# Second stage of a filter transform in groups of three columns, and a modulation vector formed later from another place

## The chip, the core and the metric

The kernel runs on one core of a Trainium2 chip, as one launch. The time is device microseconds of that core. TensorE (PE), VectorE (DVE), ScalarE (ACT), GpSimd (POOL) and SyncE (SP, here only a queue for transfers) each work through their own list of instructions, in the order in which the program emits them.

## What is computed

Two layers with a modulation taken from `c`, on 2048 positions of 640 channels, in bf16:

```
mod = (silu(c) @ w_mod) cut into sa, ca, ga, sb, cb, gb   (six vectors of 640)

h  = layernorm(x) * (1 + ca) + sa            x = A_q
ks = a causal convolution of k with 4 taps per channel (shift_k)
kv = ks * v
y  = irfft(rfft(kv, 4096) * rfft(ssm_k, 4096))[:2048] + kv * ssm_D
x  = x + ga * (h * y)

h  = layernorm(x) * (1 + cb) + sb
t  = gelu(layernorm(h) @ w1)                 640 -> 640
   shift the four quarters of t's channels by +1, -1, +2, -2 positions
x1 = h + t_shifted @ w2
o  = x1 + gelu(layernorm(x1) @ w3) @ w4      640 -> 1728 -> 640
x  = x + gb * o                              the result
```

`ssm_k` is called s below: s and kv go through the same transform, are multiplied, and go back.

## The kernel before, in words

**The long convolution.** The transform of length 4096 is done as small matrix products. For s and then for kv, 32x32 block transposes on DVE (L395) lay the data out, `stage1` (L408) makes products into T01, in two halves T0 and T1 (20480 columns in all), and stage 2 makes products of T01 with a table Gs in RG. Every stage-2 product goes to PSUM and is copied out (an eviction, by ACT at L208 or by DVE at L210), into R3 for s (called `KSX`) and into R5 for kv (`XS`). Then `inverse1` (DVE products of the two spectra at L633, matmuls at L644 and L645), `inverse2` (L685, which reads T01), and the result y in Rb.

The two stage 2 differ. That of s, `stage2` (L425), takes one column k of 32 at a time for both halves: 4 matmuls 128x320 (as 64 rows of the array at a time) into one PSUM slot and one eviction 128x640. That of kv, `stage2_half` (L446), takes one half at a time and three columns k: 12 matmuls of 160 columns and one eviction 128x960; the last of a half has two k, and 640.

**The modulation.** `mod_half` (L500 to L528) loads a 400 KB half of a column block of `w_mod`, makes its product with silu(c) (5 matmuls, L509), and puts 320 columns into `modv`. The halves i = 0 to 5 go by three early places; i = 6 to 11 (cb, then sb, then gb) use places `wl` in R3 at 0, 1600, ... 8000. The part of `modv` that holds cb, sb and gb is one region "modB", 6 to 12, to the bookkeeping.

**Second layer.** Positions are 16 tiles of 128, A0 to A15, in groups CG: [0], [1], [2], [3,4], [5,6], ... [13,14], [15] (so group 4 is A5 and A6). For a group, `chain_a` (L761 to L764) makes the new x with a sum, `chain_b` (L771 to L782, here "quick" at L775 for the first three groups, else L779 and L780) makes h, `chain_c` makes the normed h; each has a layer norm's end in `ln_finish` (L724 to L741, small POOL and DVE steps with a power on POOL at L739) and squares summed on ACT (L753). `turn` transposes a normed tile: by TensorE (L796 and a copy at L802 or L804) or, for later groups, by a DMA on SP's queue (L789, `R<-RK`). `mm_w1(g)` (L842 and L852) then multiplies a group by w1, `mm_w2` (L897, out at L904), `mm_w3` (L931, gelu at L935), `mm_w4` (L952 and L961) follow, with the output lines at L984 to L1006. `ln1_stats` and `ln1_fin` (L554 to L577) and `make_q` (L608 to L618) prepare h of the first layer tile by tile.

**Loads and places.** w3 (2160 KB, L1020) goes into the lower half of T01 and w4 (2080 KB, L1021, with two 80 KB tails at L1022 and L1023, these four in the program's order of tasks 494 to 497) into the upper half, when the transform no longer needs them. gelu's output sits in R3 (`gsf`), with zeroed edges from `gs_zero`.

**What sets the order.** `add` records a task with the regions that it reads and writes, and `run` puts all tasks in an order written out by hand, ORDER: every word is a task's number and its engine (P, A, D, G, S), and behind a colon the one to two of four PSUM slots that it takes, as in `88P:0`. Each engine gets its tasks in this order, SP's transfers too. So what is written next to what in ORDER decides who waits behind whom; the numbers given to a task as costs decide nothing at run time. A task starts when those that it depends on are done: regions that overlap, with a write among them.

Of the kernel before, what the change touches and what calls it, by code (L numbers as in the profile page):

```python
# [26 lines left out]
0S 2S 19G 18D 21G 20D 27G 29D 23D 4S 50G 28D 24A 36G 37G 22D 30A 68G 69D 25A 26G 88P:0 31A 89A 86P:1 87A 56G 90P:2 91A 72G 84P:3 5S 85A 3S 38G 39G 40A  # L27
73D 104P:0 106P:1 107A 70D 6S 49G 71D 105D 98P:2 102P:3 103A 99A 8S 118P:0 74G 94P:1 95A 75D 114P:3 115A 108P:2 109A 9S 119D 112P:0 113A 1S 66D 116P:1
41G 42G 43G 67D 80P:3 81A 117D 51D 52D 110P:2 44A 45D 10S 111D 96P:0 97A 82P:1 122P:3 11S 123D 32G 34G 54A 33S 53A 83A 76P:0 77A 100P:2 101D 92P:1 93A
78P:3 7S 120P:0 46G 136D 79A 55G 121D 175P:2 176A 47S 195P:1 196A 35S 179P:3 180A 185P:2 186D 147P:1 141P:0 193P:3 142D 148A 57G 58G 181P:2 182D 59G  # L30
139P:1 194A 140A 201S 199P:0 48S 200A 143P:3 144D 155P:2 165P:1 166D 156A 161P:0 162A 202S 191P:3 192D 12S 157P:2 158A 167P:1 168D 13S 163P:0 164A
197P:3 198A 145P:2 203S 146D 189P:1 65G 151P:0 152D 169P:3 190A 204S 183P:2 170A 184D 159P:1 160A 177P:0 178D 153P:3 154A 173P:2 174A 149P:1 150D
137P:0 260P:3 254D 171P:2 187P:1 138A 60A 188A 61G 62G 63G 261A 214D 172A 14S 124P:0 266P:1 210D 267A 125D 126P:3 127D 15S 211D 255D 209A 258P:2 259A
16S 270P:1 271A 130P:0 131D 268P:3 64A 262P:2 343G 269A 263A 215A 128P:1 264P:3 129D 256D 276P:2 277A 265A 134P:0 132P:1 17S 135D 282P:2 212A 283A
133D 216G 286P:3 223S 224P:0 220S 213G 278P:1 287D 225A 226S 279A 232S 284P:2 257D 221P:0 229S 285A 272P:3 227P:1 222A 228D 274P:2 235S 275D 273A
290P:0 291A 469D 288P:1 289A 233P:3 234D 292P:2 293A 294P:0 296P:3 230P:1 297A 298P:2 295D 299A 466D 342S 253G 246S 248G 312P:0 308P:3 309A 231D 463D
300P:1 301A 313D 460D 251G 310P:2 311D 367G 243S 306P:0 307A 316P:3 317D 280P:1 281A 252G 314P:2 304P:0 302P:3 305A 249S 240G 315D 236P:1 303A 237D
318P:2 319D 467D 340P:0 345D 241S 341A 338P:1 339A 238S 242G 326P:3 327A 344D 245S 250G 366S 322P:2 334P:0 352D 330P:1 331D 323A 244G 335A 239G 247G
324P:3 325A 346P:2 350S 351G 353D 347A 348P:0 360D 320P:3 349A 321A 328P:1 329A 354P:2 355A 359G 358S 361D 374S 356P:0 368D 369D 332P:3 333A 375G
362P:1 363A 364P:2 376D 365A 336P:3 337A 370P:1 371A 357A 372P:2 377D 378P:3 379A 380P:1 381A 383G 382S 385D 384D 386P:0 390S 391G 392D 393D 398S 373A  # L40
388P:3 387A 217A 399G 401D 394P:1 400D 425S 396P:2 397A 408D 407G 389A 402P:0 406S 409D 404P:2 395A 414S 416D 405A 415G 417D 464D 465D 426P:3 403A
427D 452S 410P:1 411A 412P:2 413A 420P:0 421D 418P:1 419A 422S 423P:3 456S 461D 470D 424D 468D 462D 218A 475P:20 477D 476A 520D 459G 454S 499D 500D
471D 521D 472A 540D 434S 219G 523D 541D 543D 437S 438P:1 439A 512A 435P:3 428S 429P:2 430A 431S 432P:0 501A 522A 433A 436A 525D 502G 504D 457S 478P:12
480A 503G 524G 526D 505D 473D 491P:03 545D 542A 544G 507D 553A 492A 527A 474D 546D 479A 571D 568D 485P:20 528G 529G 493A 530D 531P:1 506A 508G 509D
510P:3 486A 208S 547A 487A 458G 511A 548D 549G 481G 569D 570A 572D 573A 482P:20 484A 550D 551P:3 552A 532D 536P:1 533A 513D 537A 207S 574D 483D 575G
576D 580D 577D 517P:0 518A 581D 582D 583A 538P:3 578D 584G 579A 539A 585G 488P:21 489A 556P:0 557A 534D 535D 558P:3 559A 515P:2 516A 453S 514D 631D
632D 633A 586D 589D 590P:0 587P:3 455S 560P:2 634D 206S 635D 637G 591D 636A 638G 554D 561D 563D 588A 639D 562A 600P:0 601A 598P:3 599A 643D 640D 641D
642A 564G 494S 565D 644D 645D 646A 205S 441A 647D 490A 648G 566P:2 498G 567D 444D 651D 555D 605P:0 606D 607A 602P:3 649D 443D 603D 497S 652S 650S 699D
700D 447D 604A 620P:2 621A 495S 616P:1 617A 618P:0 661P:3 619A 662A 659P:2 660A 622P:1 623A 608D 609G 440D 610D 611P:0 613D 614P:3 615D 701A 663P:2
666P:1 664D 612A 683P:3 665A 667D 668A 681P:0 682A 677P:2 445G 656A 653D 654D 442G 655D 592D 669D 670G 674A 678A 671D 672P:1 673D 679P:0 680A 675P:1  # L50
593D 594D 702D 703D 496S 624P:2 595D 596D 676A 519G 597D 765D 749P:0 704A 705G 706G 766D 767A 768D 684A 707A 449A 625D 711D 747P:1 685P:32 712D 748A
769D 713D 714A 708D 709D 715D 771G 626D 446D 770A 710A 745P:1 716G 686P 717A 718S 772G 450D 719D 687D 720S 729P:3 773D 448G 750A 629S 774D 775D 777A
778D 779D 746A 727P:0 721D 781D 722D 723D 834D 835D 780A 776A 730A 627S 451G 790A 787A 657D 658D 782G 783D 743P:1 785D 791D 728A 731P:3 831D 832D 630S
688D 833A 732D 744A 733A 734P:0 735D 784S 786S 793P:1 794A 795P:3 737D 693D 694D 697S 736A 751P:02 796A 797P:1 800P:3 752P 738G 741D 836A 837G 838G
839D 753D 840D 798D 692S 739A 740S 742S 815P:0 843D 844D 801D 803D 841D 696S 813P:1 811P:3 845D 847G 842A 846A 848G 851D 788D 816A 849D 724A 725D 689S
809P:0 799A 852S 802A 804G 807D 814A 810A 812A 805D 850S 853P:1 759D 854A 808S 855P:2 856A 806S 875P:0 876A 869P:3 857P:1 873P:2 871P:0 726D 792D 874A
690S 789D 628S 754D 691S 891D 892D 894D 870A 860P:2 760D 951D 872A 895D 896A 695S 817P:30 893A 897G 898G 952D 954D 861D 862A 858D 863D 877P:21 953A
818P 903A 758S 904D 819D 899D 900D 698S 820D 859A 864G 865A 955G 905D 866S 906A 879D 822S 878P 867A 868S 933P:3 824S 901D 907G 902A 908G 909D 934A
911D 910S 956D 957D 958D 825D 912S 915P:2 935P:0 936A 913P:3 916A 763S 931P:0 757S 959A 914A 917P:2 929P:3 932A 960G 930A 961G 756S 821S 823S 962D
755S 963S 966P:0 967A 918D 919A 826D 885D 886D 920P:2 921D 830S 888S 829S 923G 762S 764S 922A 964P:1 965A 937P:30 969P:2 761S 880D 924G 968G 970D  # L60
972P:1 1003P:2 939D 925A 881S 1004D 926S 973D 975G 927A 928S 987P:3 988A 983P:2 971A 981P:1 890S 984A 1006G 974A 1005A 883S 889S 882S 827S 982A 985P:3
828S 976G 977D 1007G 938P 945D 979A 1008A 978S 980S 1010P:2 1011A 1012P:1 884S 1009S 946D 949S 1016P:0 1017A 948S 940D 942S 944S 1014P:2 943S 986A
# [75 lines left out]
def kernel(  # L138
# [277 lines left out]
    def stage2(XSd, dreg):  # L416
        for k in range(32):
            ps = Slot()

            def f(e, ps=ps, k=k):  # L420
                psv = pst(ps, name="ps_s2")[:, :, 0:320].rearrange("p g (h s) -> p g h s", h=2)
                for cc in range(2):
                    for g in range(2):
                        p = slice(64 * g, 64 * g + 64)
                        nc.tensor.matmul(psv[:, g], lhsT=Gs[p, k, 64 - 64 * cc:192 - 64 * cc], rhs=T1b[p, cc * 32 + k],  # L425
                                         start=(cc == 0), stop=(cc == 1), tile_position=(64 * g, 0))
            t0 = add("PE", 0.275, f, r=[("T01", 0, 20480), ("RG", 192 * k, 192 * k + 192)], alloc=ps, ni=8)
            w = [(dreg, 0, 20480, "s2")]
            if dreg == "R5":
                w += [("kT", 0, 5, "s2"), ("vT", 0, 5, "s2"), ("kTp", 0, 1, "s2")]  # L430
# [658 lines left out]
```

## Time and profile before

| | us |
|---|---|
| median of 3 runs | 305.56 |
| lowest and highest | 305.46, 309.11 |
| the profiled execution | 305.2 |
| its span (first to last instruction) | 303.4 |

The mean clock that TensorE was granted in the profiled execution is 0.971 of full. In the profile a line is a number of the kernel before; "L208 ACT CAST R<-ps_s" is a copy by ACT from the PSUM tile ps_s into R (R3 and R5 both are R, buffer numbers being left out; Ra, Rb, RG, RH, RK and RQ keep their letter). "x36" counts instructions, "128x960 bf16<-128x960 f32" is an instruction's shape. SPq is the issuing of a DMA by SP, "DMA" in a chain of waits is the transfer itself up to its landing.

By time, the span falls into: 0 to 8 us set-up; 8 to 28 stage 1 of s; 28 to 40 stage 2 of s; 40 to 60 the shift of k and stage 1 of kv; 60 to 97 stage 2 of kv and the inverse; 97 to 142 the layer norms and first products of the second layer; 142 to 303 the products with w1 to w4.

### The profile page before, as it was taken

To read this page: it belongs to the slowest core of one execution; us is meant where nothing else is said; L and a number is where in the kernel's file an instruction comes from. 1 tells how busy PE (TensorE), PEld (TensorE's weight loads), DVE (VectorE), ACT (ScalarE), POOL (GpSimd) and SP (SyncE) were. 2 spreads that over 40 slices of the span, in tenths; PEclk is the share of its full clock that TensorE was granted. 3 is DMA by queue.
4 is the path that set the end of the run, shared out by engine and by line. 5 is a ranking of instruction groups with operands and counts; after the bars stand their busy time and mean duration, and the time that the engine had idled before them with its cause. 6 is when DMAs were issued, how large, how long until landed. Compare 5 with 4: busy or idle time off the path is not lost.

```text
span 303.4 us, 7652 instructions
## 1 busy us (share of the span) xinstructions
PE 270.4 (89%) x3054; PEld 206.8 (68%) x3054; DVE 217.9 (72%) x432; ACT 209.9 (69%) x352; POOL 112.2 (37%) x251
## 2 busy tenths in 40 slices
PE   0989999998989738788999998999999999999993
PEld 0655655877878426667887676788867886887761
DVE  8998999999999998789769985746464054032342
ACT  4789999999999989887678677275760762714110
POOL 4978562362214874421544752130242131300000
PEclk9999999999999956799999999999999999999999
DMA  6998999797799910824600311223014023130111
GB/s 217 262 196 186 219 192 229 211 247 224 192 256 276 283 26 3 286 64 99 239 2 1 47 39 32 54 54 67 2 27 88 22 53 76 27 83 2 37 47 43
DMA packets 58115, 35.75 MB, mean 118 GB/s; under 512 B 39872, under 2 KB 54848, under 8 KB 58080
## 3 DMA queue, kind: packets, MB, share of 16 engines
q1 hardware_dynamic: 56768, 31.55, 43.5%
q0 software_dynamic: 1216, 3.67, 4.5%
q8 instruction: 24, 0.39, 0.5%
q14 instruction: 11, 0.09, 0.1%
q10 hardware_dynamic: 96, 0.04, 0.1%
HBM read 16.31 MB, written 2.62 MB: 62 GB/s over the span
## 4 chain that ended last, share of the span: by engine, by line
PE 57%; DVE 13%; POOL 8%; DMA 8%; ACT 6%; issue 5%; SPq 1%; DVEq 0%; POOLq 0%; ACTq 0%
PE ps_w L931 17%; PE ps_w L961 15%; PE ps_ksh L480 5%; PE ps_w L842 4%; PE ps_w L897 4%; PE ps_s L408 4%; DVE Rb L633 3%; ACT R L208 3%; POOL lnv L739 2%; DMA R<-RK 2%; DMA Rb<-R 2%; PE ps_i L644 2%; PE ps_i L645 2%; DMA RK<-R 2%; DVE R L780 1%
## 5 line engine op out<-in xcount | busy, mean ns | idle before, releaser
L931 PE MATMUL ps_w<-R,T 128*128 128x256 bf16 (+1 forms) x630 | 64.6, 261 | 0.9 <-DMA R<-RH 0.7
L935 ACT ACTIVATE R<-ps_w 128x1024 bf16<-128x1024 f32 (+2 forms) x36 | 29.0, 829 | 47.2 <-PE ps_w L931 47.1
L931 PEld LDWEIGHTS <-T 128*128 128x128 bf16 x630 | 55.6, 98 | 8.5 <-issue 2.4
L961 PE MATMUL ps_w<-T,R 128*128 128x320 bf16 x416 | 59.0, 299 | 0.0
L961 PEld LDWEIGHTS <-R 128*128 128x128 bf16 x416 | 40.2, 98 | 15.6 <-issue 0.5
L208 ACT CAST T<-ps_s 128x1024 bf16<-128x1024 f32 x34 | 32.7, 1027 | 3.3 <-PE ps_s L408 3.3
L753 ACT ACTIVATE RG<-R 128x640 bf16<-128x640 bf16 x32 | 23.5, 735 | 13.4 <-DVE R L780 9.1
L408 PE MATMUL ps_s<-F1bd,Rb 128*128 128x256 bf16 x160 | 22.6, 292 | 9.0 <-DVE Rb L395 8.9
L984 DVE TENSOR_TENSOR T<-ps_w,R 128x640 bf16<-128x640 f32 x15 | 12.3, 822 | 22.2 <-PE ps_w L952 11.5
L208 ACT CAST R<-ps_s 128x640 bf16<-128x640 f32 (+1 forms) x36 | 27.4, 844 | 1.1 <-PE ps_s L425 0.6
L408 PEld LDWEIGHTS <-Rb 128*128 128x128 bf16 x160 | 16.4, 104 | 15.0 <-DVE Rb L395 9.6
L739 POOL TENSOR_TENSOR lnv<-lnv,mhalf 128x2 f32<-128x2 f32 (+1 forms) x29 | 23.2, 799 | 2.3
L897 PE MATMUL ps_w<-RG,R 128*128 128x320 bf16 x160 | 23.4, 299 | 0.3 <-ACT R L844 0.3
L842 PE MATMUL ps_w<-R,RG 128*128 128x256 bf16 (+1 forms) x200 | 21.2, 269 | 1.4 <-DMA R<-RK 0.8
L726 POOL TENSOR_SCALAR lnv<-stat 128x2 f32<-128x2 f32 (+1 forms) x14 | 4.9, 349 | 44.3 <-DVE Ra L764 17.2
L842 PEld LDWEIGHTS <-RG 128*128 128x128 bf16 x200 | 18.2, 107 | 3.7 <-issue 2.1
L904 DVE SCALAR_TENSOR_TENSOR R<-ps_w,R 128x640 bf16<-128x640 f32 x16 | 12.9, 818 | 10.3 <-PE ps_w L897 10.3
L644 PE MATMUL ps_i<-EA,Rb 128*128 128x128 bf16 x160 | 19.2, 220 | 1.0 <-DVE Rb L633 0.8
L645 PE MATMUL ps_i<-EB,Rb 128*128 128x128 bf16 x160 | 19.0, 219 | 0.8 <-DVE Rb L633 0.6
L897 PEld LDWEIGHTS <-R 128*128 128x128 bf16 x160 | 15.3, 98 | 6.5 <-ACT R L844 0.6
L738 POOL TENSOR_TENSOR lnv<-stat,lnv 128x2 f32<-128x2 f32 x19 | 4.0, 212 | 40.5 <-ACT RG L753 29.8
L480 PE MATMUL ps_ksh<-R,RQ 128*128 128x512 bf16 x80 | 18.8, 380 | 0.1
(179 smaller groups left out, 536.1 us busy)
## 6 DMA issues: line engine op xcount, KB each, us to landing
Ra<-in_A_ssm_k_dram SPq DMA_DIRECT2D x5, 512.0 KB, 5.2
Ra<-in_A_q_dram SPq DMA_DIRECT2D x8, 320.0 KB, 6.0
R<-in_w_mod_dram SPq DMA_DIRECT2D x6, 400.0 KB, 5.3
out_dram<-RH SPq DMA_DIRECT2D x60, 40.0 KB, 1.6
T<-in_B_w_dram SPq DMA_DIRECT2D x1, 2160.0 KB, 9.0
T<-in_B_w_dram SPq DMA_DIRECT2D x1, 2080.0 KB, 10.1
RH<-in_w_mod_dram SPq DMA_DIRECT2D x4, 400.0 KB, 5.2
RK<-R SPq DMA_DIRECT2D x5, 256.0 KB, 3.2
```

The source lines that it names most:

```text
L208: nc.scalar.copy(dst, src(ps.tile))
L408: nc.tensor.matmul(psv[:, ml, :], lhsT=xL[:, s0:s0 + P], rhs=F1r, start=True, stop=True)
L480: nc.tensor.matmul(pt[:, i, :], lhsT=diagw[:, b, jj, :], rhs=kT[:, b, c0:c0 + 512], start=(jj == 0), stop=(jj == 3))
L644: nc.tensor.matmul(psv[:, w, :], lhsT=Av[:, r_, :, g_], rhs=EAf, start=True, stop=False)
L645: nc.tensor.matmul(psv[:, w, :], lhsT=Bv[:, r_, :, g_], rhs=EBf, start=False, stop=True)
L739: nc.gpsimd.tensor_tensor(rs, rs, mhalf[:, 0:n], ALU.pow)
L753: add("ACT", 0.74, lambda e: nc.scalar.activation(junk, src, ACT.Square, scale=float(D) ** -0.5, accum_out=stat[:, li, 1, t:t + 1]), r=[sk ...
L842: nc.tensor.matmul(pt[:, fb, 0:cw], lhsT=w1_sb[:, b, 160 * fb:160 * fb + P], rhs=hT[:, b, 0:cw], start=(b == 0), stop=(b == ND - 1))
L897: nc.tensor.matmul(pt[:, hf, 0:320], lhsT=gsf[:, fb, c0:c0 + P], rhs=w2_sb[:, fb, 320 * hf:320 * hf + 320], start=(fb == 0), stop=(fb == 4))
L931: nc.tensor.matmul(pt[:, fl, 0:cw], lhsT=w3_sb[:, b, fb * P:(fb + 1) * P], rhs=xT[:, b, 0:cw], start=(b == 0), stop=(b == ND - 1))
L935: nc.scalar.activation(g3[g % 2][:, f0:f0 + fn, 0:cw], ps.tile[:, 0:fn, 0:cw], ACT.Gelu_apprx_tanh)
L961: nc.tensor.matmul(bank(i, hf), lhsT=gg[:, fb, i * P:(i + 1) * P], rhs=w4_sb[:, fb, 320 * hf:320 * hf + 320], start=(fb == 0 and i == 0), ...
```

## The change

- `stage2` is gone. s goes through `stage2_half(KSX, "R3", h)` for both halves: 22 tasks in place of 32, with 12 (at a half's end 8) matmuls of 160 columns each and evictions of 128x960 (at a half's end 128x640).
- The bookkeeping of "modB" is split: `chain_b` depends on cb and sb alone (6 to 10), the output lines on gb (10 to 12).
- The two halves of gb load into R5 (13824 and 15424) in place of R3 (6400 and 8000).
- A cost of the planner is another (0.17 to 0.145 per k), which decides nothing at run time.
- ORDER is written anew as a whole (1036 tasks in place of 1056). A task behind stage 2 of s has a number lower by 20. Among other things, the order of the last transfers on SP before the products' stage is another, and so is the order of some statistics, `make_q` and norm tasks on DVE and ACT.

SP's tasks around the loads of w3 and w4, in words of ORDER, with what they are:

```
before: 494S w3   205S x rows  497S tail of w4  652S turn A6   650S turn A5  495S w4       496S tail of w4
after:  187S x rows  434S piece of w2 474S w3   632S turn A6   475S w4       630S turn A5  476S 477S tails of w4
```

The diff without ORDER, cut:

```diff
-    def stage2(XSd, dreg):
-        for k in range(32):
...
-            t1 = evac(XSd[:, :, k, :], lambda t: t[:, :, 0:320].rearrange("p g x -> p x g"), 640, ps, w)
-    def stage2_half(h):
+    def stage2_half(XSd, dreg, h):
         for k0 in range(0, 32, 3):
             kn = min(3, 32 - k0)
...
-            t0 = add("PE", 0.17 * kn, f, r=[("T01", 10240 * h, 10240 * h + 10240), ("RG", 192 * k0, 192 * (k0 + kn))], alloc=ps, ni=8 * kn)
-            w = [("R5", 10240 * h, 10240 * h + 10240, "s2"), ("kT", 4 * h, 5, "s2")] + ([("vT", 0, 5, "s2")] if h else [("kTp", 0, 1, "s2")])
-            t1 = evac(XS[:, 160 * h:160 * h + 160, k0:k0 + kn, :],
+            t0 = add("PE", 0.145 * kn, f, r=[("T01", 10240 * h, 10240 * h + 10240), ("RG", 192 * k0, 192 * (k0 + kn))], alloc=ps, ni=8 * kn)
+            w = [(dreg, 10240 * h, 10240 * h + 10240, "s2")]
+            if dreg == "R5":
+                w += [("kT", 4 * h, 5, "s2")] + ([("vT", 0, 5, "s2")] if h else [("kTp", 0, 1, "s2")])
+            t1 = evac(XSd[:, 160 * h:160 * h + 160, k0:k0 + kn, :],
                       lambda t, kn=kn: t[:, :, 0:480].rearrange("p g (k s) -> p s k g", k=3)[:, :, 0:kn], 320 * kn, ps, w)
...
-    stage2(KSX, "R3")
+    for h in range(2):
+        stage2_half(KSX, "R3", h)
...
-    wl = [(R3[:, o:o + 1600].rearrange("p (b n) -> p b n", b=ND), ("R3", o, o + 1600)) for o in range(0, 9600, 1600)]
+    wl = [(R3[:, o:o + 1600].rearrange("p (b n) -> p b n", b=ND), ("R3", o, o + 1600)) for o in range(0, 6400, 1600)]
+    wl += [(R5[:, o:o + 1600].rearrange("p (b n) -> p b n", b=ND), ("R5", o, o + 1600)) for o in (13824, 15424)]
...
-                    u, x_all[:, A, :], nm[:, i:i + 1], cb1, ALU.add, ALU.mult), r=[xk_(A), nk, ("modB", 6, 12)], w=[uk], port=0.8)
+                    u, x_all[:, A, :], nm[:, i:i + 1], cb1, ALU.add, ALU.mult), r=[xk_(A), nk, ("modB", 6, 10)], w=[uk], port=0.8)
...
-            add("DVE", 1.02, f, r=[xk_(t), ("modB", 6, 12)], w=[bk, ok], port=0.8)
+            add("DVE", 1.02, f, r=[xk_(t), ("modB", 10, 12)], w=[bk, ok], port=0.8)
```

More of the change, by code (lines that the diff above doesn't have):

```diff
@@ L26 @@
 ORDER = """
[L27 to L62, printed above, removed]
@@ L63 @@
-989P:03 887S 1013A 1036P:1 991D 992D 996S 994S 1038P:0 990P 1015A 947S 997D 1034P:2 1039A 941S 1018P:03 1035A 1032P:2 1033A 998D 999S 1001S 993S 1002S
-1042D 1043D 1000S 950S 1020D 1021D 1025S 1024S 1022S 1023S 1019P 1026D 1037A 995S 1027D 1031S 1029S 1030S 1028S 1040P:02 1044D 1045D 1047S 1046S 1048S
-1049S 1041P 1050D 1051D 1052S 1053A 1054S 1055A
+18D 19G 2S 27G 20D 28D 31A 21G 23D 29D 22D 36G 30A 37G 0S 68G 69D 24A 25A 26G 86P:0 87A 88P:1 89A 84P:2 85A 38G 39G 4S 72D 73D 102P:3 103A 90P:0 50G
@@ new lines @@
+5S 74D 6S 104P:1 8S 106P:2 75D 108P:3 49G 91D 40A 116P:0 41G 107A 109A 1S 42G 66D 67D 9S 117D 112P:2 110P:3 105A 100P:1 32D 76P:0 113A 52D 118P:2 101A
+51D 53A 54A 3S 70D 111A 114P:1 10S 120P:3 43G 44A 71D 45D 115A 77A 92P:1 93A 119D 11S 121D 82P:2 83D 78P:0 79A 33G 34G 94P:3 95A 47S 46S 96P:1 97D
+80P:2 136D 81A 56G 12S 57G 58G 59G 60A 98P:0 99A 122P:3 157P:1 158A 123D 153P:2 154A 149P:0 150D 175P:1 55G 176A 35S 61G 62G 155P:3 156D 137P:2 138A
+48S 151P:0 152A 181S 143P:1 183S 144D 7S 165P:3 166A 147P:2 184S 161P:0 145P:1 148D 162A 159P:3 160A 146D 63G 139P:2 140A 163P:0 164A 141P:1 142A
@@ new lines @@
+126P:3 234D 238P:2 239A 246P:0 247A 124P:1 64A 182S 191D 190D 179P:2 180A 171P:0 13S 127D 177P:3 169P:2 172A 125D 170A 65G 167P:1 235D 178A 168A 14S
+130P:0 254P:2 255A 248P:3 194D 15S 131D 189D 249A 195A 128P:1 16S 256P:2 240P:0 192A 129D 236D 17S 134P:3 241A 135D 193G 132P:1 133D 173P:0 257A 174A
+200S 201P:3 202A 203S 252P:2 253A 188S 237D 242P:1 243A 204P:0 205D 264P:3 262P:2 265A 263D 272P:1 273A 276P:0 277D 270P:3 322S 244P:2 245D 446D
+250P:1 206S 274P:0 275D 323G 271A 282P:3 296P:2 251A 207P:1 208D 283A 449D 280P:3 297A 212S 213P:0 214D 209S 281A 288P:1 298P:2 289A 443D 299D 346S
@@ new lines @@
+294P:3 215S 295A 284P:0 285D 268P:1 269A 278P:2 279D 266P:3 210P:0 211D 267A 260P:1 258P:2 261A 231G 440D 259D 292P:3 293A 290P:0 291D 286P:1 287A
+216P:2 320P:3 304P:0 321A 305A 233S 217D 441D 228S 316P:1 317A 308P:2 302P:3 303A 347G 310P:0 309A 311A 306P:1 307A 324D 325D 328P:3 312P:2 313A 332D
+444D 326P:0 327A 230S 232G 218G 222S 318P:1 319A 329D 224G 300P:3 221S 226S 220G 229S 227S 223G 225G 219S 330S 331G 333D 334P:2 335A 336P:0 337A 340D
+338S 339G 341D 342P:1 348D 301A 344P:2 314P:0 343A 315A 345A 349D 350P:3 352P:1 351A 353A 196G 354S 356D 355G 357D 363G 360P:0 197A 358P:2 359A 362S
@@ new lines @@
+364D 365D 366P:3 367A 371G 368P:1 369A 370S 373D 372D 361A 379G 378S 374P:2 386S 376P:3 377A 375A 380D 381D 384P:1 385A 388D 387G 389D 382P:0 383A
+405S 396D 406P:3 394S 395G 397D 402S 447D 198D 439G 392P:2 393A 390P:1 407D 391A 398P:0 399A 432S 433S 400P:2 401A 448D 445D 442D 438G 403P:1 404D
+452D 450D 455P:30 199G 457A 453D 435S 456D 479D 480D 492A 408S 409P:2 481A 411S 412P:1 500D 513A 520D 501D 185S 410A 413A 502A 521D 503D 482G 484D
+505D 523D 417S 522A 454D 471P:03 472A 483G 485D 525D 458P:21 460A 437S 504G 506D 459A 524G 526D 528D 186S 473A 486A 507A 527A 508D 487G 488G 436S 414S
@@ new lines @@
+415P:0 416A 509G 465P:12 467A 529G 461G 489D 490P:3 466A 491A 187S 418P:0 451D 548D 510D 511P:2 512A 530D 531P:1 551D 552D 419D 497P:3 498A 532D
+518P:2 553A 549D 550A 514D 515D 462P:01 463A 464A 519A 536P:3 538P:0 539A 537A 495P:1 493D 494D 421D 434S 468P:20 554G 555G 556D 560D 557D 561D 558D
+559A 516P:3 562D 564D 611D 563A 565G 569D 496A 570P:1 566D 614D 470A 612D 615D 517A 567P:0 568D 571D 613A 616A 540P:3 541D 580P:0 543D 542A 581A
+578P:1 579A 423D 617G 474S 618G 623D 469A 619D 624D 544G 545D 546P:3 620D 625D 585P:0 626A 621D 622A 582P:1 478G 547A 602P:2 627G 420D 427D 628G 629A
@@ new lines @@
+631D 603A 632S 586D 587A 600P:3 583D 422G 598P:0 588D 584A 589G 599A 596P:2 601A 590D 591P:1 593D 475S 594P:0 630S 639P:3 640A 592D 641P:1 642A 533D
+534D 595D 657P:0 663P:3 424D 664A 425G 597A 426D 636D 535D 679D 680D 643P:1 476S 681A 644D 572A 645A 646P:3 647D 648A 573D 574D 682D 683D 684A 428G
+704A 477S 604P:2 659P:1 605D 649G 685D 658A 650G 654D 686G 651D 652P:3 653A 655P:2 656D 633A 660A 661P:0 729P:3 727P:2 725P:1 662A 730A 665P:03 687D
+688D 689D 575D 690A 691D 692D 693D 694A 429A 695D 696G 697D 728A 430A 698S 726A 699D 700S 709P:2 710A 701D 634D 702D 703D 707P:1 708A 431G 576D 635D
@@ new lines @@
+748D 749D 814D 750A 577D 667D 745D 746D 747A 606D 751G 752G 723P:0 724A 637D 815D 816A 638D 811D 812D 817G 609S 813A 818G 711P:2 712D 714P:1 715D 607S
+716A 713A 717D 731P:02 666P 753D 754D 755D 732P 757A 705D 758D 718G 719A 720S 668D 671S 733D 721A 722S 793P:1 759D 760A 819D 820D 761G 756A 821D 822A
+762G 765A 766S 823D 824D 825D 826A 770D 789P:0 763D 767D 610S 673D 674D 827G 706D 871D 794A 771D 764S 828G 829A 672S 608S 830S 775P:3 776A 831D 669S
+772D 739D 832S 773P:1 774A 872D 790A 734D 736S 737S 873A 791P:2 780P:3 781D 835P:1 792A 768D 782A 677S 836A 777P:0 778D 783D 779A 670S 784G 795P:2
@@ new lines @@
+796A 931D 932D 769D 874D 875D 876A 833P:3 834A 785D 787D 788S 797P:01 877D 878G 883A 933A 837P:2 884D 786S 675S 740D 743S 838D 839A 678S 840P:3 841D
+842A 799D 843G 844G 847D 848S 845D 846S 885D 855P:2 856A 853P:3 879D 880D 798P 881D 676S 805D 849P:0 850A 934G 935G 936D 915P:2 851P:1 741S 937D
+909P:0 916A 911P:2 499G 854A 886A 735S 852A 857P:31 887G 882A 888G 912A 938D 939A 910A 738S 891D 806D 892S 889D 890S 895P:2 896A 893P:0 894A 913P:2
+800D 859D 808S 940G 941G 744S 914A 942D 943S 946P:3 947A 944P:0 945A 948G 742S 897P:2 898D 899A 900P:3 901D 860D 863S 949P:0 903D 902A 904G 907D
@@ new lines @@
+952P:2 953D 905D 983P:3 984D 986D 950D 951A 858P 865D 917P:23 802S 985A 908S 906S 967P:0 963P:1 987G 988A 955D 919D 954A 956G 957D 961P:2 959D 964A
+989S 803S 965P:1 918P 966A 804S 801S 862S 866D 925D 962A 868S 869S 958S 960S 992P:1 993A 968A 994P:2 996P:3 997A 995A 810S 990P:1 1014P:0 991A 864S
+861S 926D 928S 809S 807S 969P:32 1018P:1 920D 971D 921S 923S 870S 930S 970P 1019A 977D 1012P:3 998P:12 1022D 1023D 867S 1015A 1016P:0 927S 924S 922S
+978D 979S 981S 980S 982S 929S 972D 975S 974S 1000D 1001D 1005S 1013A 1002S 973S 1003S 976S 1004S 999P 1006D 1007D 1008S 1010S 1009S 1011S 1017A
@@ L66 @@
+1020P:31 1024D 1025D 1026S 1027S 1029S 1028S 1021P 1030D 1031D 1035A 1032S 1033A 1034S
 """
@@ L414, in stage1 @@
             pl.tasks[-2].succ.append(pl.tasks[-1])
-    def stage2(XSd, dreg):
-        for k in range(32):
[L418 to L430, printed above, removed]
-            t1 = evac(XSd[:, :, k, :], lambda t: t[:, :, 0:320].rearrange("p g x -> p x g"), 640, ps, w)
-            dep(t1, t0)
-    def stage2_half(h):
+    def stage2_half(XSd, dreg, h):
         for k0 in range(0, 32, 3):
@@ L437, in stage2_half, with f @@
             ps = Slot()
-            def f(e, ps=ps, k0=k0, kn=kn):
+            def f(e, ps=ps, k0=k0, kn=kn, hh=h + (2 if dreg == "R5" else 0)):
                 psv = pst(ps, name="ps_s2")[:, :, 0:480].rearrange("p g (k s) -> p g k s", k=3)
@@ L600 @@
     for h in range(2):
-        stage2_half(h)
+        stage2_half(XS, "R5", h)
     qring = [RQ[:, i * D:(i + 1) * D] for i in range(5)]
@@ L775, in chain_b @@
                 add("DVE", 0.82, lambda e, u=u, A=A, i=i: nc.vector.scalar_tensor_tensor(
-                    u, x_all[:, A, :], nm[:, i:i + 1], cb1, ALU.add, ALU.mult), r=[xk_(A), nk, ("modB", 6, 12)], w=[uk], port=0.8)
+                    u, x_all[:, A, :], nm[:, i:i + 1], cb1, ALU.add, ALU.mult), r=[xk_(A), nk, ("modB", 6, 10)], w=[uk], port=0.8)
             else:
                 normed(u, uk, x_all[:, A, :], xk_(A), rn, i)
-                add("DVE", 0.48, lambda e, u=u: nc.vector.tensor_tensor(u, u, cb1, ALU.mult), r=[("modB", 6, 12)], w=[uk], port=0.8)
+                add("DVE", 0.48, lambda e, u=u: nc.vector.tensor_tensor(u, u, cb1, ALU.mult), r=[("modB", 6, 10)], w=[uk], port=0.8)
             add("DVE", 0.82, lambda e, u=u, A=A, i=i: nc.vector.scalar_tensor_tensor(
                 h_all[:, A, :], u, rs[:, i:i + 1] if quick else 1.0, sbv, ALU.mult, ALU.add, accum_out=stat[:, 1, 0, A:A + 1]),
-                r=[uk, lk, ("modB", 6, 12)], w=[hk_(A), ("s1", 100 + A, 101 + A)], port=0.8)
+                r=[uk, lk, ("modB", 6, 10)], w=[hk_(A), ("s1", 100 + A, 101 + A)], port=0.8)
             square_sum(h_all[:, A, :], hk_(A), 1, A)
@@ L997, in last_tile @@
         rl, rk = R5[:, 17408:17408 + D], ("R5", 17408, 17408 + D)
-        add("DVE", 0.48, lambda e: nc.vector.tensor_tensor(rl, h_all[:, t, :], gbv, ALU.mult), r=[hk_(t), ("modB", 6, 12)], w=[rk], port=0.8)
+        add("DVE", 0.48, lambda e: nc.vector.tensor_tensor(rl, h_all[:, t, :], gbv, ALU.mult), r=[hk_(t), ("modB", 10, 12)], w=[rk], port=0.8)
         add("DVE", 0.48, lambda e: nc.vector.tensor_tensor(rl, rl, x_all[:, t, :], ALU.add), r=[xk_(t)], w=[rk], port=0.8)
@@ L1005, in last_tile @@
             t1 = add("DVE", 0.48, lambda e, c=c, hf=hf: nc.vector.tensor_tensor(bo[:, c], pss[hf].tile[:, hf, 0:320], gbv[:, c], ALU.mult),
-                     r=[("modB", 6, 12)], w=[bh], use=pss[hf])
+                     r=[("modB", 10, 12)], w=[bh], use=pss[hf])
             dep(t1, td)
```

## Prediction

> **What bounds the kernel now.** I read the page first (busy shares, slices, chain), then the windows stage by stage, then the chain of waits and SyncE's queue around 140 us, where the change's new order differs most.
>
> ```profile
> span 303.4 us, 7652 instructions
> PE 270.4 (89%) x3054; PEld 206.8 (68%) x3054; DVE 217.9 (72%) x432; ACT 209.9 (69%) x352; POOL 112.2 (37%) x251
> PEclk9999999999999956799999999999999999999999
> ```
> ```profile
> 28.00:40.00 12.00, 11.42 (x133) 6.83 (x130) 11.49 (x15) 11.64 (x19) 6.57 (x10) 1.00 1.11 218
> 97.00:112.00 15.00, 8.42 (x340) 5.38 (x339) 14.27 (x36) 13.71 (x29) 11.86 (x21) 0.76 0.75 195
> 112.00:128.00 16.00, 11.55 (x286) 10.15 (x287) 13.55 (x35) 14.14 (x32) 7.34 (x25) 0.71 0.32 112
> 142.38:160.00 17.62, 17.61 (x165) 14.91 (x166) 12.74 (x37) 12.81 (x24) 7.81 (x26) 1.00 0.38 127
> 160.00:190.00 30.00, 28.70 (x236) 21.74 (x233) 24.42 (x63) 22.61 (x45) 14.43 (x31) 1.00 0.17 30
> 190.00:240.00 50.00, 49.88 (x414) 39.24 (x411) 26.50 (x66) 26.41 (x49) 11.25 (x33) 1.00 0.22 47
> 240.00:260.00 20.00, 19.30 (x171) 14.99 (x170) 8.87 (x19) 9.32 (x18) 4.72 (x19) 1.00 0.23 52
> ```
> The columns are stretch, length, then busy time and instructions of PE, PEld, DVE, ACT, POOL, then granted clock, DMA share, GB/s. Three regimes: until 97 us DVE and ACT are both full (the evictions of the transform); from 97 to 142 us nobody is full, a chain of small steps sets the time and TensorE's clock is low; from 142.38 us TensorE is full, with 1.30 + 0.12 + 0.70 = 2.1 us idle up to 260 us. So whatever delays TensorE after 142 us delays the end.
>
> ```profile
> 139.22 0.36 DVE RK L610
> 139.61 2.64 DMA R<-RK
> 142.25 0.14 issue
> 142.38 0.71 PE ps_w1x L852 x5
> ```
> ```profile
> 121.84 0.38 SPq L1020 DMA_DIRECT2D T<-in_B_w_dram  x1
> 122.27 1.25 SPq L540 DMA_DIRECT2D Ra<-in_A_q_dram  x1
> 123.62 0.64 SPq L1023 DMA_DIRECT2D T<-in_B_w_dram  x1
> 138.10 2.71 SPq L789 DMA_TRANSPOSE R<-RK  x2
> 140.87 0.57 SPq L1021 DMA_DIRECT2D T<-in_B_w_dram  x1
> 141.50 0.94 SPq L1022 DMA_DIRECT2D T<-in_B_w_dram  x1
> ```
> ```profile
> DMA to landing us min/median/max: 10.1/10.1/10.1
> ```
> The first is the chain at the gate of the TensorE-bound part: A5's normed tile (L610), its transpose by DMA, then `mm_w1` of group 4. The second is SyncE's own queue: the transposes of A6 (138.10) and A5 (139.61), and only behind them the 2080 KB w4 load (L1021, 140.87), which the third line says took 10.1 us to land. Every load of that queue in this trace lands in the order of issue, small ones late behind large ones: the 80 KB tail of w4 (L1022) took 9.7 us, issued at 141.50; a tile's turn in an empty queue took 2.64 us.
>
> **The change, part by part.**
>
> *Stage 2 of s in threes.* Before: 32 evictions 128x640, 20 on ACT at 0.648 us busy and 12 on DVE at 0.77: 12.96 + 9.24 = 22.2 us on two engines that the window 28 to 40 shows full (11.49 and 11.64 of 12). After: 20 of 128x960 and two of 128x640, by the new order 17 on ACT and 5 on DVE; at 0.927 and 1.12 us (rows of the kv half) at most 17 x 0.927 + 5 x 1.12 = 21.4. The gain is 0.8 us of engine time, 0.4 us of path. TensorE gets 256 matmuls of 160 columns for 128 of 320; the 256 of the kv stage (L446) were busy 10.4 us, against 11.2 for L425, and lie under the evictions. The new order has one more `ln1_stats`, mod eviction and `make_q` on DVE before 97 us, about 1 us, so the front moves by -1.5 to +1; I take -0.5.
>
> *gb formed later, from R5.* In 97 to 112 us two mod halves of gb leave the way: an ACT eviction (0.7 us), and TensorE's wait of 0.61 us at L685 for it. The order also moves A7's `ln1_stats` (ACT 97.32 to 98.9, on the chain of waits) to DVE and lets POOL's `ln1_fin` start some 3 us sooner. I take -2.5 for the first norm groups, between 0 and -3.5 (the whole ACT and POOL head of that chain). That wait's cover: nothing reads gb before the output lines at 150 us and later, so its late forming costs nothing. `gs_zero` and the gelu no longer wait for these halves in R3; no row shows such a wait, so 0.
>
> *The rewritten order: w4 between two turns.* This is the largest term. SyncE's order before is turn A6, turn A5, w4, tails. After it is turn A6, **w4**, turn A5, tails. w4 (2.08 MB) has nothing to wait for: the last inverse2 matmuls that read its place are far ahead. A5's turn is issued behind w4 in the same queue, and `mm_w1` of group 4 stands in TensorE's order ahead of all w3, w2 and w4 work of groups 1 and later. TensorE runs in order, so it waits.
> - A6's turn: 138.10 before; -3.0 (the two gains above), +2.2 for two more `ln1_stats` (2 x 1.09) that DVE now does between A6's shift and its norm: 137.3. Bounds 135.5 to 139.5.
> - w4 issued 1.4 us later (turns took 1.51 and 1.26 us of issue): 138.7. Landing 10.1 us later as in before, where it also followed a turn: 148.8. Lower bound 8.6 us, the w3 load's 8.98 scaled by 2080/2160.
> - A5's turn lands behind it: bounds 0.2 us (the tail's landing behind w4, 151.22 against 151.01) and 2.64 (undisturbed); 1.2, about the spacing of two turns: 150.0. TensorE starts 0.1 us later, as at 142.25 to 142.38: 150.1, against 142.38.
> - From there before took 303.43 - 142.38 = 161.05 us. The new order has done one w3 piece (0.56) and two turns by TensorE (0.68) by then: 159.8. Sum 309.9.
> - The clock: TensorE is idle some 7 us. Before, the clock fell to 0.5 at 104.78 and at 125.26 after 3.4 us of about half-empty TensorE, and stayed there in pieces of 3.4 us. At 0.5, twenty L842 matmuls took 2.29 us (125.53) against 1.29 (121.71), so a piece of 3.4 us loses 3.4 x (1 - 1.29/2.29) = 1.5 us. One piece +1.5; bounds 0 and 3.0.
> - Given back: DVE, ACT and POOL run ahead in the pause, so some of the 2.1 us that TensorE idled later can go: -1.2, bounds 0 and -2.1.
>
> Sum: 309.9 + 1.5 - 1.2 = 310.2 us of span; 1.8 us lie around it (305.2 for a span of 303.4), so **312.0 us**. The profiled execution's 305.2 is 0.4 under the median 305.56; that is within what the runs differ by.
>
> A rule that speaks against this: the Trainium skill's "DMA: Bandwidth & Descriptors", section "Queues, rings and completion order", says that each ring is consumed in order but that completion is not first-in-first-out per issuing engine. Taken as leave for A5's small turn to land before w4, it would give the sum of rival 1 below. This trace shows no such overtaking among SyncE's loads (the 9.7 us tail above), and the measurement decides.
>
> **The rivals.**
> 1. *The turn is not held by w4* (ends not slower). For: a turn is a transpose on a path of its own, and no turn in before was issued right behind a large load; the only transposes behind loads are the first k and v tiles, the first issued at 4.07 us behind four 512 KB loads and landed at 12.31. Against: that same 8.2 us. Then A5 lands 2.64 us after an issue at about 139.3: 142.0, gate at 142.1, end 142.1 + 159.8 = 301.9, minus some 0.9 recovered: 301 + 1.8 = 302.8. The turning point is the landing of A5's turn against the moment TensorE has done its w3 pieces and w2 turns, about 142.
> 2. *The stall, and two pieces of half clock* or the turn of A6 not earlier: + 1.5 each: 313.5 to 315.
> 3. *The change does nothing measurable*: w4 is issued early, because A6's chain gains its full 3.5 us and the statistics hide, and lands at 145.5; then gate 146.8, end 306.6 + 0.4, with the slack fully returned 305: 306.8 us.
>
> **How the numbers follow.** Stall as worked out (309.5 to 313): 0.57. Rival 2: 0.15. Rival 3 (304.5 to 309.5): 0.13. Rival 1: 0.15. The likeliest case's own range is 309.5 to 313.5. The range of 303 to 315.5 takes in the others. Two per cent, about what a measurement of this kernel tells from no change, are 299.4 and 311.7. Slower by over 2%: a little over half of the likeliest case and all of rival 2: 0.48. Faster by over 2% would need 6 us, more than rival 1 with every bound in its favour but a little: 0.04. Within 2%: 0.48.
>
> **What would show it.** In the changed kernel: on SyncE's queue the w4 load between two turns, A5's turn taking near 11 us to land instead of 2.64; on TensorE one wait of 6 to 8 us for DMA R<-RK ahead of group 4's `mm_w1` (L842 or L852 before), its first matmul near 150; a clock of 0.5 for 3 to 7 us around it. ACT and DVE sums for the s stage 2 of 21 us instead of 22, and a first norm chain about 2.5 us sooner. I am wrong if A5's turn lands within 4 us of issue, if w4 is issued before 136, or if TensorE finds work ahead of the gate; and wrong on the small terms if the front moves by more than 1.5 us.

## The result, and the profile after

| | before | changed |
|---|---|---|
| median, us | 305.86 | 315.0 |
| lowest to highest | 305.46 to 309.11 | 314.13 to 316.01 |
| ratio to before, with 95% interval | | 1.0285 [1.0215, 1.0355] |
| profiled execution, us (span) | 305.2 (303.4) | 314.13 (312.4) |

The change makes the kernel 2.85% slower (the ratio is not the quotient of the two medians, which is 1.030; the two agree within the interval). 312.0 was forecast, so the forecast was right in sign and mechanism and 3 us short. From the second layer on, line numbers of the changed kernel are lower by 15 than before's (L842 is L827, L852 is L837, L789 is L774, L1021 is L1006).

The page of the changed kernel:

```profile
span 312.4 us, 7890 instructions
PE 272.4 (87%) x3178; PEld 209.7 (67%) x3182; DVE 219.6 (70%) x443; ACT 203.7 (65%) x332; POOL 112.2 (36%) x241
PEclk9999999999999659699599999999999999999999
```

TensorE's busy time rose by 2.0 us only (270.4 to 272.4), the span by 9.0, so TensorE is idle 7 us longer. Where, its waits from 97 us on say (in total, times, the longest):

```profile
PE ps_mod L493 <- DMA R<-in_w_mod_dram: 6.9, 3, 4.2
PE ps_w L827 <- DMA R<-RK: 6.0, 1, 6.0
```

The first was one wait of 0.5 us before (L509 there). The second is the forecast one. SyncE's queue of the changed kernel around it (start, time to issue):

```profile
141.30 1.28 SPq L774 DMA_TRANSPOSE R<-RK  x1
142.68 0.52 SPq L1006 DMA_DIRECT2D T<-in_B_w_dram  x1
143.36 3.08 SPq L774 DMA_TRANSPOSE R<-RK  x1
146.50 0.58 SPq L1007 DMA_DIRECT2D T<-in_B_w_dram  x1
```

A6's turn, w4, A5's turn. The time from issue to landing of the turns by this line of code, shortest, median and longest:

```profile
DMA to landing us min/median/max: 2.6/2.6/8.7
```

The longest, 8.70 us, is A5's: issued at 143.36, it landed at 152.06, 0.63 us behind w4, which landed at 151.43 (8.75 after issue). Even the issue of that turn took 3.08 us instead of the usual 1.2. And TensorE:

```profile
142.06 2.39 PE L916 MATMUL ps_w<-R,T 128*128 128x128 bf16 x40 [0.24 <-DVE R L889]
145.39 0.81 PE L781 MATMUL ps_tr<-RG,RH 128*128 128x128 bf16 x10 [0.94 <-DVE RH L733]
152.20 3.74 PE L827 MATMUL ps_w<-R,RG 128*128 128x256 bf16 x20 [6.00 <-DMA R<-RK]
155.77 0.71 PE L837 MATMUL ps_w1x<-R,RG 128*128 128x256 bf16 x5
```

TensorE has its w3 pieces and turns done at 146.20 and stands for 6.00 us; its first `mm_w1` of group 4 begins at 152.20 (142.38 before, forecast 150.1), and takes 3.74 us for twenty matmuls instead of 2.35, because the granted clock is 0.5 from 148.26 to 155.09 (the 5 in the twentieth of the 40 slices of PEclk, 148.4 to 156.2 us). From there to the end it takes 160.2 us.

### The profile page after: what moved, and what is told of

It is laid out like the page before. It is cut to its first block, busy times and chain, and to the rows that moved or that the text cites. A ratio compares the mean times of both kernels' runs of the same rounds, so it can differ in the third digit from the quotient of the medians.

```text
span 312.4 us, 7890 instructions
## 1 busy us (share of the span) xinstructions
PE 272.4 (87%) x3178; PEld 209.7 (67%) x3182; DVE 219.6 (70%) x443; ACT 203.7 (65%) x332; POOL 112.2 (36%) x241
## 5 line engine op out<-in xcount | busy, mean ns | idle before, releaser
L207 ACT CAST T<-ps_s 128x1024 bf16<-128x1024 f32 x32 | 30.7, 1022 | 3.9 <-PE ps_s L407 3.4
L207 ACT CAST R<-ps_s 128x960 bf16<-128x960 f32 (+1 forms) x35 | 31.3, 973 | 1.9 <-PE ps_s L427 1.4
L827 PE MATMUL ps_w<-R,RG 128*128 128x256 bf16 (+1 forms) x200 | 21.9, 273 | 7.2 <-DMA R<-RK 6.0
L827 PEld LDWEIGHTS <-RG 128*128 128x128 bf16 x200 | 18.1, 107 | 9.9 <-issue 7.7
L427 PE MATMUL ps_s<-T,RG 64*128 64x160 bf16 x512 | 21.5, 230 | 1.9 <-DVE R L468 0.9
L724 POOL TENSOR_TENSOR lnv<-lnv,mhalf 128x2 f32<-128x2 f32 (+1 forms) x29 | 21.8, 751 | 2.3
L427 PEld LDWEIGHTS <-RG 64*128 64x128 bf16 x512 | 17.7, 94 | 6.3 <-issue 5.0
L723 POOL TENSOR_TENSOR lnv<-stat,lnv 128x2 f32<-128x2 f32 x19 | 5.5, 291 | 43.4 <-ACT RG L738 37.9
```

The costliest lines, as they stand in the source:

```text
L207: nc.scalar.copy(dst, src(ps.tile))
L427: nc.tensor.matmul(psv[:, g, j], lhsT=Gs[p, k, 64 - 64 * cc:192 - 64 * cc], rhs=T1h[h][p, cc * 32 + k], start=(cc == 0), stop=(cc == 1), t ...
L724: nc.gpsimd.tensor_tensor(rs, rs, mhalf[:, 0:n], ALU.pow)
L827: nc.tensor.matmul(pt[:, fb, 0:cw], lhsT=w1_sb[:, b, 160 * fb:160 * fb + P], rhs=hT[:, b, 0:cw], start=(b == 0), stop=(b == ND - 1))
```

## The experiments

Each ratio is to the kernel before, on the same chip, with its 95% interval.

**A5's turn ahead of w4**

```diff
-... 631D 603A 632S 586D ... 593D 475S 594P:0 630S 639P:3
+... 631D 603A 632S 630S 586D ... 593D 475S 594P:0 639P:3
```

> The changed kernel with one word of ORDER moved: A5's turn (630) directly behind A6's (632), ahead of the w4 load (475). Theory 'the queue's order makes the stall': A5's turn is issued about 142.7 us and lands about 145.4; TensorE, which has its earlier pieces done at 146.2, waits under 0.5 us instead of 6.0, the half-clock piece that cost 1.4 us at the restart is gone, and of the sum of 7.4 us up to 1.5 is lost again to pauses that the stall had hidden: span 305 to 307, 307 to 309 us. Rival 'the gate is held by something else' (A6's own turn, or the statistics): the wait stays 4 to 6 us under another name and the time 313 to 315 us.

306.92 us, 1.0034 [1.0001, 1.0067]. SyncE's queue, then TensorE:

```profile
141.45 2.66 SPq L774 DMA_TRANSPOSE R<-RK  x2
144.16 0.57 SPq L1006 DMA_DIRECT2D T<-in_B_w_dram  x1
```
```profile
145.54 0.81 PE L781 MATMUL ps_tr<-RG,RH 128*128 128x128 bf16 x10 [0.93 <-DVE RH L733]
146.18 1.04 PE L827 MATMUL ps_w<-R,RG 128*128 128x256 bf16 x8
```

Both turns go out back to back, A5's lands 2.60 us after its issue, and `mm_w1` follows the turn before it without a wait, at 146.18, where the changed kernel began at 152.20. A6's turn goes out at 141.45, as in the changed kernel. One word of ORDER carries some 8 of the 9 us.

**w4 between the turns, in the kernel before**

```diff
-... 652S 650S 699D ... 621A 495S 616P:1 ...
+... 652S 495S 650S 699D ... 621A 616P:1 ...
```

> The kernel before with one word of ORDER moved: the w4 load (495) between the two turns (652 and 650). Theory 'the queue's order': w4 issued 139.6, landed 8.7 us later at 148.3, A5's turn at 148.9, the gate at 149.1 instead of 142.38: 6.7 us later, plus 1.4 us of half clock, less up to 2 us of later pauses: 310 to 313.5 us. Rival 'a turn is not held by a load in front of it': 305 to 306 us. Rival 'the loss of the changed kernel comes mainly from its later norm chain': under 309 us.

315.82 us, 1.0293 [1.0254, 1.0332]: the whole loss of the change, made in the kernel before with the same word.

```profile
139.87 1.28 SPq L789 DMA_TRANSPOSE R<-RK  x1
141.20 0.57 SPq L1021 DMA_DIRECT2D T<-in_B_w_dram  x1
141.88 3.31 SPq L789 DMA_TRANSPOSE R<-RK  x1
```
```profile
150.97 1.22 PE L852 MATMUL ps_w1x<-R,RG 128*128 128x256 bf16 x5 [8.01 <-DMA R<-RK]
151.99 3.73 PE L842 MATMUL ps_w<-R,RG 128*128 128x256 bf16 x20
```

The signature is the same: the turn's issue 3.31 us, its landing 8.95 after issue, one wait of 8.01 us, and 3.73 us for the twenty matmuls of L842, most of them at the low clock. It cost more than the 310 to 313.5 expected. A6's turn, which nothing in this edit touches, went out 1.8 us later than in the profiled execution of before (139.87 against 138.10). And from the gate to the end it took 162.9 us instead of 161.05: the low clock cost 1.9 us (1.4 on L842, 0.5 on the five matmuls of L852), and nothing was given back.

**w4 by GpSimd's queue**

```diff
-    dma("SP", 2200, w3t[1], ...
+    dma(("SP", "POOL"), 2200, w3t[1], ...
-... 593D 475S 594P:0 630S
+... 593D 475G 594P:0 630S
```

> The changed kernel with the w4 load issued by GpSimd's queue instead of SyncE's, at the same place of ORDER. Theory 'order within SyncE's queue': A5's turn shares the transfer engines with w4 but not the queue, lands 3 to 5 us after its issue, and TensorE waits at most 2 us: 307 to 311 us. Rival 'the transfer engines are full, whoever issues': A5's turn still takes 7 to 9 us to land and the time is 313 to 316 us.

308.4 us, 1.0074 [1.0032, 1.0116]; A5's turn landed 2.59 us after its issue. But it does not tell the two theories apart: GpSimd works through its own list in order, and sent w4 only behind its norm steps, at 145.31, when A5's turn (issued 143.26) was half a microsecond from landing.

```profile
144.65 0.70 POOL L724 TENSOR_TENSOR lnv<-lnv,mhalf 128x2 f32<-128x2 f32 x1
145.31 1.28 POOL L1006 DMA_DIRECT2D T<-in_B_w_dram  x1
```

Whether a turn next to w4 on another queue would land early stays open; that it is late behind w4 in one queue, the first two runs show.

**Threes alone, in the kernel before.** `stage2` becomes `stage2_half` for s, nothing else; first in 22 of the old 32 places of ORDER, then with the four PSUM places in rotation and 12 evictions on ACT, 10 on DVE in turn.

```diff
-    stage2(KSX, "R3")
+    for h in range(2):
+        stage2_half(KSX, "R3", h)
```

> The kernel before with the second stage of s in threes per half and nothing else: 22 of the 32 places of its tasks in ORDER are kept (15 evictions on ACT, 7 on DVE), all else stays in place. Theory 'evictions bound this stage': 15 x 0.927 + 7 x 1.12 = 21.7 us of engine time instead of 22.2, so 0.2 to 0.5 us less: 304.5 to 306. Rival 'twice the matmuls at half the width make TensorE the bound there': 1 to 2 us more, 306.5 to 308.

309.94 us, 1.0105 [1.0065, 1.0145]: slower than either side expected.

> The kernel before with the second stage of s in threes and nothing else, as in the run that took 309.9, but with the four PSUM places in rotation and 12 evictions on ACT, 10 on DVE in turn, where that run kept the old places: there TensorE waited seven times 0.2 to 0.7 us for a place to come free, and DVE idled between its evictions. Theory 'that run lost by its places and engines, not by the groups of three': stage 2 of s ends at 39.5 to 40.5 us as in the kernel before, and the time is 304.5 to 306.5. Rival 'groups of three are slower in themselves' (fewer, longer pieces on four places): stage 2 ends after 41 us again and the time is 307.5 to 310.

307.02 us, 1.0004 [0.9963, 1.0045], between the two expectations. The window of 28 to 40 us (busy time of PE, PEld, DVE, ACT, POOL), the first with old places, then the one in rotation (whose profiled execution was the slowest of its twelve, 309.72 us, so it speaks for the stage and not for the time):

```profile
28.00:40.00 12.00, 8.96 (x224) 7.74 (x219) 8.03 (x8) 10.19 (x12) 6.56 (x10) 1.00 1.10 208
```
```profile
28.00:40.00 12.00, 11.05 (x262) 9.39 (x257) 11.77 (x12) 10.35 (x12) 6.58 (x10) 1.00 1.10 204
```

With the old places DVE worked 8.03 of 12 us: TensorE waited up to 0.73 us at a time for a place, and DVE for TensorE. In rotation both run. So groups of three are not slower in themselves, and are worth nothing that this measurement can see; how places and engines are dealt out is worth 1%.

**The load of w2 behind those of the modulation** (with A5's turn ahead)

```diff
-... 398P:0 399A 432S 433S 400P:2 ... 436S 414S 415P:0
+... 398P:0 399A 432S 400P:2 ... 436S 414S 433S 415P:0
```

> The changed kernel with A5's turn ahead of w4 (as in the run of that kind before) and, on SyncE's queue, the 700 KB load of w2 (433) moved behind the last load for the modulation (414), as in the kernel before. Theory 'queue order also costs the norm chain': TensorE's waits for a modulation load in the chain stage, 4.3 to 6.9 us in three pieces, fall under 2 us in all, A6's turn is issued 1 to 3 us sooner than 141.45, and the time is 304 to 306 us. Rival 'DVE is the bound of that stage' (14.7 of 15 us busy from 97 to 112 us): the waits go and nothing is gained: 306.5 to 307.5 us.

306.46 us, 1.0003 [0.9967, 1.0039], so nothing beside 1.0034 [1.0001, 1.0067] without it. The waits for these loads fell as expected, from 4.3 us in three pieces to the second line below. But TensorE ran no sooner: its matmuls of `inverse2` (L670) now stood idle for as long, the first line. There "issue" means that the profile shows nothing they waited for.

```profile
PE ps_i L670 <- issue: 4.3, 2, 2.4
PE ps_mod L493 <- DMA R<-in_w_mod_dram: 0.5, 1, 0.5
```

A6's turn went out at 141.80, no sooner. This fits the rival: DVE was busy for 9.7 of the 10 us from 105 to 115, here and without the move. That DVE sets the time there is argued from this and not shown.

**gb formed later still** (with A5's turn ahead): first only its first half behind its second, then that with w2's load, then both halves behind the turns of A3 and A4.

```diff
-... 414S 415P:0 416A 509G ... 419D 497P:3 ...
+... 414S 509G ... 419D 415P:0 416A 497P:3 ...
```

> The changed kernel with A5's turn ahead of w4 and the product and eviction of gb's first half (415, 416) moved behind those of its second half (419), so that inverse2 of tiles A5 to A7 no longer stands on TensorE behind the load of that half. Theory 'the late load of gb stops TensorE': the wait of 2.8 to 4.2 us near 111 us goes, tiles A3 and A4 get through 1 to 3 us sooner, 304.5 to 306 us. Rival 'DVE is the bound of that stage': 306.5 to 307.5 us.

309.21 us, 1.0057 [1.0017, 1.0097].

> The changed kernel with all three moves: A5's turn ahead of w4, w2's load behind the modulation's, gb's first half formed behind its second. Theory 'queue order costs the norm chain': the better of the two runs or up to 1 us less, 303.5 to 305.5 us. Rival 'DVE is the bound there': 306.5 to 307.5.

308.55 us, 1.0065 [1.003, 1.01].

```diff
-... 415P:0 416A ... 418P:0 ... 419D ... 568D 571D 613A ...
+... 568D 571D 418P:1 419D 415P:1 416A 613A ...
```

> The changed kernel with A5's turn ahead of w4 and all of gb's products and evictions (415, 416, 418, 419) moved behind the turns of A3 and A4 (571), where TensorE waits anyway. In the changed kernel DVE evicts gb's second half at 116.3 us, ahead of A3's new x at 117.75, and TensorE waits up to 4.2 us for the load of its first half. Theory 'gb's forming stands in the norm chain': A3's x 1 to 1.5 us sooner after the first x, A6's turn 1 to 2 us sooner than 141.45, 305 to 306 us. Rival 'the chain's own steps set it, gb fills gaps': 306.5 to 308 us.

313.35 us, 1.0227 [1.0151, 1.0304]. All three are slower than the kernel before, and than either side expected. What the first move costs is clearest between 308.55 and 306.46 us, two runs on one chip that differ by it alone. In the last of the three, TensorE's product of gb waits for a PSUM place that a turn's copy holds, and `mm_w2`, the eviction on DVE and group 4's norm queue behind it (TensorE, then DVE):

```profile
133.52 0.85 PE L493 MATMUL ps_mod<-R,silu_w 128*128 128x320 bf16 x5 [2.21 <-DVE R L789]
134.96 0.98 PE L493 MATMUL ps_mod<-R,silu_w 128*128 128x320 bf16 x5 [0.58 <-DVE modv L506]
```
```profile
138.64 0.82 DVE L889 SCALAR_TENSOR_TENSOR R<-ps_w,R 128x640 bf16<-128x640 f32 x1 [3.74 <-PE ps_w L882]
```

That eviction is at 132.72 in the run with only the turn moved, and A6's turn is 6 us later for it, at 147.38. Ahead of that nothing was gained either: group 3's `chain_b` came 21.0 us after the first new x, and 20.7 us in the run with only the turn moved. So these traces do not show that the change lost time by where it put gb.

**The first loads in the old order** (with A5's turn ahead): s's block 3 ahead of the first k tile, the first v tile ahead of block 1; then this with gb behind the chain, then with w2's load moved.

```diff
-... 5S 74D 6S ... 109A 1S 42G 66D 67D 9S ... 54A 3S 70D
+... 5S 3S 74D 6S ... 109A 9S 1S 42G 66D 67D ... 54A 70D
```

> The changed kernel with A5's turn ahead of w4 and the first loads on SyncE's queue in the order of the kernel before: s's fourth block (3) ahead of the first k tile's transpose, and the first v tile's transpose (9) ahead of s's first block (1). In the changed kernel the second v tile landed at 22.8 to 24.9 us, before at 21.2, and DVE waited 0.2 to 2.3 us for it at L468. Theory 'queue order also costs at the front': it lands near 21.2, the front is 0 to 2 us sooner, 304.5 to 306.3 us. Rival 'a wait there is made up by 97 us': 306.5 to 307.5 us.

309.31 us, 1.0094 [1.0057, 1.013].

> The changed kernel with A5's turn ahead of w4, gb behind the chain and the first loads in the old order. If the two parts add: 303 to 305 us. If the norm chain takes up what the front gives: as the better of the two alone, 305 to 306.

314.82 us, 1.0261 [1.0195, 1.0326].

> The changed kernel with A5's turn ahead of w4, w2's load behind the modulation's and the first loads in the old order: all of SyncE's queue mended. Theory 'what the change loses beside A5's turn is lost in this queue': 304 to 305.5 us. Rival 'the chain's own steps set it': 306 to 307 us.

309.14 us, 1.0095 [1.0061, 1.013]. All three are slower than expected. In the first of them the second v tile did land sooner than with only the turn moved (22.09 instead of 24.93), but s's block 1, now behind the first v tile, landed at 17.63 instead of 13.70, and DVE's order wants that block first:

```profile
17.65 0.61 DVE L444 TENSOR_TENSOR Ra<-Ra,Dcol 128x1 bf16<-128x1 bf16 x1 [3.31 <-DMA Ra<-in_A_ssm_k_dram]
```

The last DVE product of the inverse began 2.8 us later (99.12 against 96.31). No version beat the kernel before beyond its interval; the nearest are the changed kernel with the turn ahead and w2's load moved (1.0003) and threes in rotation (1.0004).

## Why the prediction was right, and which terms were not

- **The time.** 315.0 us lies outside the likeliest case's own 309.5 to 313.5, and the forecast gave a loss of over 2% no more than 0.48. What was right is the mechanism; part of the closeness is opposite errors that cancel, as the terms show.
- **The stall: right.** w4 between two turns held A5's turn, and TensorE with it: shown by taking the word out (1.0285 to 1.0034) and by putting it into the kernel before (to 1.0293).
- **Its terms.** w4's landing was taken as 10.1 us and was 8.75; A5's turn behind it as 1.2 us and was 0.63. For w4 the lower bound of 8.6 us was the better guess. In the two runs with w4 between the turns it landed 8.75 and 8.97 us after issue; in the eleven where SyncE sent it behind both turns, 9.76 to 10.38. Why is not shown: in before and in the changed kernel alike a turn was still under way when w4 was issued.
- **A6's turn at 137.3: wrong, the term that made the forecast short.** It went out at 141.30, outside the bounds of 135.5 to 139.5. The gains of 3.0 us that this term took (-0.5 for the front, -2.5 for the first norm groups) did not come, nor did the loss of 2.2 us by two more `ln1_stats`. Against before, the inverse's last product ended 1.5 us later (95.85 against 94.31), the stretch from the first new x to group 3's `chain_b` took 22.0 us instead of 19.4, the stretch from there to the turn 16.7 instead of 17.8. Against the forecast that is +2.0 for the front, +5.3 up to `chain_b` (with 0.2 us ahead of the first new x) and -3.3 behind it, together +4.0. The two opposite errors, +4.0 here and -1.9 for landings, make the gate's +2.1. Part of the 4.0 is the spread between executions: with before's order up to this turn it went out at 138.10 and, in the run with w4 between the turns, 139.87; with the changed order at 141.30 to 141.81 in four runs (changed, turn ahead, w4 by GpSimd, w2's load moved).
- **What was read wrong ahead of it.** The prediction said of 97 to 142 us that nobody is full. Its own rows have DVE busy for 14.27 of the 15 us from 97 to 112 (95%), and 13.55 of 16 to 128. A gain taken from single ACT and TensorE pieces had little room there.
- **Why the first norm groups gained nothing.** `chain_b` no longer depends on gb, but the new order puts other work there. The squares of A3 and A4 on ACT, before and then after:

```profile
114.81 0.74 ACT L753 ACTIVATE RG<-Ra 128x640 bf16<-128x640 bf16 x1
115.67 0.74 ACT L753 ACTIVATE RG<-Ra 128x640 bf16<-128x640 bf16 x1
118.78 1.28 ACT L844 ACT_TABLE_LOAD   x1
```
```profile
117.51 1.28 ACT L843 ACT_TABLE_LOAD   x1
118.81 1.11 ACT L843 ACTIVATE R<-ps_w1x 32x128 bf16<-32x128 f32 x4
119.94 0.74 ACT L738 ACTIVATE RG<-Ra 128x640 bf16<-128x640 bf16 x1
```

  Before, they ran ahead of the change of table, the first 0.6 us after A4's new x began; after, they stand behind it and a gelu, 2.2 us after that x. A4's new x is itself 1.8 us later, counted from the first new x (15.1 against 13.3 us): on DVE gb's second half is evicted ahead of it (116.31), and a turn copied (117.34). That this order is the cause of the 2.6 us is read from the trace and was not tried; the same stretch took 20.7 us with only the turn moved, so about half of the 2.6 is within the spread of executions. Taking away the waits for the modulation's loads brought A6's turn no further forward, as the run with w2's load moved shows.
- **Threes: 0.4 us of path forecast,** none measured, within [-0.37%, +0.45%], 1.1 to 1.4 us either way. The front of the changed kernel was 1.5 us later, beyond the bound of +1; in six more executions of its first part the inverse's last product ended 0.1 to 2.1 us later still (95.98 to 97.94).
- **From the gate to the end: right in sum.** 160.1 forecast (159.8 + 1.5 - 1.2), 160.2 measured. The clock's piece was 3.74 - 2.35 = 1.4 us against 1.5. The low clock lasted 6.8 us, two of the forecast's pieces, but all of it up to 152.20 lay in the wait and cost nothing; that about one piece was left over is luck. The reading that the clock fell after 3.4 us of half-empty TensorE does not hold for both places in before: TensorE was idle for 1.0 us of the 3.4 ahead of 104.78, and for 1.8 of those ahead of 125.26. Given back was less than the 1.2 us: TensorE's idle time behind the gate fell from 7.3 us (161.05 less 153.73 busy) to 6.7 (160.23 less 153.53).
- **Rival 1, a turn not held by w4,** is refuted by 8.70 us against 2.6; so is, for this case, the reading of the Trainium skill's "DMA: Bandwidth & Descriptors", section "Queues, rings and completion order", as leave to overtake. The section's other half, that a ring is consumed in order, agrees with what was measured: A5's turn landed 0.63 us after w4. In each of the fourteen profiled kernels SyncE's 156 to 159 transfers landed in the order of their issue. **Rival 2** (a later A6, 313.5 to 315) is where the time fell, by A6 and not by a second piece of low clock under load. **Rival 3** is refuted: w4 went out at 142.68, not early.

## What to carry to other kernels

A small transfer that an in-order engine waits for costs what stands in front of it in its queue, not its own size (here 8.7 us instead of 2.6): where a list of tasks decides the order, read the transfers' queue as one more engine, and look for a large load that has time, directly ahead of a small one that has none. A gap in the queue order can be roughly priced beforehand from two rows, the large load's landing and the moment the waiting engine runs dry. And a wait seen in the profile is worth removing only if nothing else fills the same stretch: taking 4 us of waits for loads off TensorE only put as much other idle time beside a full DVE, and moving gb behind the chain or the first loads into another order put a new wait elsewhere.

## What the runs showed of the hardware that was not expected

- A transpose issued behind the 2 MB load held the queue's issue itself for 3.08 and 3.31 us; the median of these turns is 1.2.
- The same twenty matmuls of 128x256 took 3.74 us, not twice the 2.35 at full clock, since the clock rose again 2.9 us into them. While the granted clock was 0.5 they started 0.213 us apart, at full clock 0.110 us, so almost the whole factor of two was paid.
- With the changed order of the first loads, the second v tile landed between 22.8 and 24.9 us in seven executions of it, against 20.8 to 21.2 in four with the order before: one and the same list of transfers can end 2 us apart. DVE waited for it for 0.2 us in the changed kernel and 2.3 us in the run with only the turn moved.
